# Reordering the opening of a routed expert kernel: exponentials behind four more evictions, copies on GpSimd, the first one-hot matrix ahead of the table, scatters regrouped

## The chip, the cores and the metric

The kernel runs on one core of one Trainium2 chip. The metric is device time in microseconds (us). Before the change the median of three runs is 1338.36 us (1338.25 to 1338.87). The profiled execution has a span of 1355.9 us; times inside the kernel are counted from the start of that span.

The engines are TensorE (PE; its weight loads are listed as PEld), VectorE (DVE), ScalarE (ACT), GpSimd (POOL) and SyncE (SP, which here only issues DMAs and reads registers). Each engine runs its own queue in order; they wait for each other through semaphores.

## What is computed

The input has 8 sequences of 3584 tokens of 192 floats. First a causal convolution over 7 taps, with softmaxed taps of one of 8 heads for each group of 24 channels. Then every token goes to one of 8 experts:

```python
logits = x @ w_gate;  local_gate = sigmoid(x @ w_local)
e = argmax(logits[s]) if s == 0 or local_gate[s] < 0.5 else prev_e   # carries along the sequence
p = softmax(logits[s])
out[s] = p[e] * (relu(x[s] @ w1[e]) @ w2[e])        # w1: 192 x 1024, w2: 1024 x 192
```

All of it is float32. The choice carries on from token to token, so routing is a scan along the sequence.

## The kernel before

**Parts and blocks.** The 28672 tokens are handled in 16 parts of 1792. A part is convolved, its logits are formed, it is routed (each token gets a row in a table of slots in DRAM, sorted by expert), and its rows are scattered into `slots` by GpSimd's indirect DMAs (`put`, line 761; 16 scatters for each of the first two parts). The expert work goes block by block: a block is 128 (later 256) tokens of one expert. For a block, SyncE loads the expert's weights (`load_w`, line 890, 1536 KB, into one of four `wb` buffers) and the rows from `slots` (`load_rows`, line 900). TensorE then turns the rows (`turn`), multiplies by w1 (`hidden`, line 951) and by w2 (`output`, line 968), and the result is scattered to the output.

**The opening.** The first two parts are convolved another way, on TensorE with a banded matrix: `wide` (line 191) is a generator with 23 yields that makes 16 matmuls of one head and one half each (`convolve`, line 203), turns the result (`turned`), copies some columns (`again`, line 217), and multiplies by the gate (`products`). In part 0 (`both` true) ScalarE and VectorE share the evictions from PSUM and GpSimd makes the copies of `again`. In part 1 (`both` false) ScalarE makes all evictions and the copies too. `wide_route` (line 391) is a second generator that routes such a part: the maximum of the logits, `ex = lg - max`, the keys (line 412 reads `ex`), the exponential on ScalarE that writes over `ex` (line 415), a transpose on TensorE (line 422), the scans over tokens on VectorE (lines 435 to 448), a transpose back (line 450), one-hot experts and their counts (lines 460 to 465), the running count `upto` (line 472), and the slot of each token, `pos`.

The driver (line 1058 on) interleaves them by hand. This order is the order of every engine's queue, since the scheduler is manual:

```python
for n in (7, 5, 1, 0, 0):
    next(route0)          # one stage of the routing of part 0
    some(wide1, n)        # n pieces of the convolution of part 1
puts_behind(None, 4)      # four scatters of part 0
rest(route0)              # first_table, hots(0)
some(wide1, WIDE - 17)
```

**The first table.** `first_table` (line 496) turns the counts into the table of the first blocks: which rows and which expert block i has (`tabi`, line 518). SyncE reads `tabi` before it can issue `load_w` for blocks 0, 1 and 2 (nine DMAs, line 897). The second half of the function forms `rel`, from which `hots(0)` (line 538) makes a one-hot matrix in four instructions. With it TensorE gathers the rows of block 0 straight from the chip's own memory (`gather`, line 544), with no detour through `slots`. Block 1 is gathered the same way with `hots(1)`.

**The scatters.** The 16 scatters of part 0 stand on GpSimd's queue in five groups. Four come first; then three behind the logits of part 1 (`mark["lt", 1]`, line 271), two behind `nf` (line 435), two behind `oh` (line 460) and five behind `upto` of part 1 (line 472). `load_rows` of block 2, the first that reads `slots`, waits for all 16. On SyncE's queue the weights of block 3 stand behind that load.

**PSUM buffers.** The matmuls of the opening all write to a pool of four `hps` buffers. TensorE's queue is in order, so a matmul that waits for a buffer to be evicted holds back every later one, those of the routing included.

Of the kernel before, what the change touches and what calls it, by code (L numbers as in the profile page):

```python
# [17 lines left out]
P = 128  # L18
# [5 lines left out]
UT = 128  # L24
# [42 lines left out]
def bcast(ap, n):  # L67

    return ap.rearrange("p (a o) -> p a o", o=1).to_broadcast([ap.shape[0], ap.shape[1], n])
# [8 lines left out]
def kernel(  # L78
# [112 lines left out]
    def wide(g, xv, y_sb, both):  # L191

        lps = yps_p.tile([P, 512], F32, name="yps")[:, :4 * TB].rearrange("p (q s) -> p q s", s=TB)
        count = [0]

        def mine():
            count[0] += 1  # L200
            return both and count[0] % 2 == 0

        def convolve(half, heads):
            bs = slice(half * NH, (half + 1) * NH)
            for h in heads:
                ps = hps_p.tile([P, 512], F32, name="hps")[:TB, :NH * GS]
                nc.tensor.matmul(ps, lhsT=hank[:NI, h, :],  # L207
                                 rhs=xv[:NI, bs, h * GS:(h + 1) * GS], start=True, stop=True)
                to = y_sb[:TB, bs, Y0 + h * GS:Y0 + (h + 1) * GS]
                at = ps.rearrange("p (b d) -> p b d", d=GS)  # L210
                if mine():
                    nc.vector.tensor_scalar(to, at, rz[:TB, h:h + 1], None, Alu.mult)
                else:
                    nc.scalar.activation(to, at, Act.Copy, scale=rz[:TB, h:h + 1])  # L214
                yield

        def again(half):
            bs = slice(half * NH, (half + 1) * NH)
            copy = nc.gpsimd.tensor_copy if both else nc.scalar.copy
            copy(yr[:, bs, :], y_sb[:TB, bs, Y0 + P:Y0 + D])  # L220
            copy(y_sb[:TB, bs, Y0 + D:IX], y_sb[:TB, bs, Y0:Y0 + DR])

        def turned(half, qs):
            at = half * 3 * NH // 2
            for q in qs:
                tps = hps_p.tile([P, 512], F32, name="hps")[:, :4 * TB].rearrange(
                    "p (u s) -> p u s", s=TB)
                for u in range(4):
                    b = half * NH + (q * 4 + u if q < 2 else 2 * u)
                    src = (y_sb[:TB, b, Y0:Y0 + P] if q < 2  # L230
                           else yr[:, b:b + 2, :].rearrange("p b d -> p (b d)"))
                    nc.tensor.transpose(tps[:, u, :], src, identity=ident[:TB, :TB])
                leave = nc.vector.tensor_copy if mine() else nc.scalar.copy
                leave(yT[:, at + 4 * q:at + 4 * q + 4, :], tps)
                yield

        def products():
            for j in range(4):
                u = j // 2 * 3 * NH // 2 + j % 2 * 4
                nc.tensor.matmul(lps[Q * j:Q * j + Q], lhsT=wgb[:, 0, :], rhs=yT[:, u:u + 4, :],  # L240
                                 start=True, stop=False, skip_group_check=True)
            for i in range(2):
                for j in range(4):
                    u = j // 2 * 3 * NH // 2 + NH + j % 2 * 2
                    nc.tensor.matmul(lps[Q * j:Q * j + Q, i::2, :], lhsT=wgb[:, 1 + i, :],
                                     rhs=yT[:, u:u + 2, :], start=False, stop=(i == 1),
                                     skip_group_check=True)

        yield from convolve(0, range(H))
        zy = z_tile()  # L250
        yT = zy[:, :3 * NH * TB].rearrange("p (u s) -> p u s", s=TB)
        yr = zy[:TB, 3 * NH * TB:].rearrange("p (b d) -> p b d", d=DR)
        again(0)
        yield from convolve(1, range(5))
        yield from turned(0, (0, 1))
        yield from convolve(1, range(5, H))
        yield from turned(0, (2,))
        again(1)
        yield from turned(1, range(3))
        products()  # L260
        if both:
            nc.vector.tensor_copy(lsb[:, :2, :], lps[:, :2, :])
            nc.scalar.copy(lsb[:, 2:, :], lps[:, 2:, :])
        else:
            nc.scalar.copy(lsb, lps)
        yield
        ltp = yps_p.tile([P, 512], F32, name="yps")[:TB].rearrange("p (q c) -> p q c", c=P)
        for q in range(4):
            nc.tensor.transpose(ltp[:, q, :], lsb[:, q, :], identity=ident)
        lt = sm.tile([P, NB, E + 1], F32, name="lt")[:TB]  # L270
        mark["lt", g] = nc.vector.tensor_copy(lt.rearrange("p (j q) e -> p j q e", q=4),
                              ltp.rearrange("p q (j c) -> p j q c", c=Q)[:, :, :, :E + 1])
        got[g] = lt
# [117 lines left out]
    def wide_route(g, y_sb, lt):  # L391
# [15 lines left out]
        nc.vector.tensor_reduce(mx, lg, axis=AX.X, op=Alu.max)  # L407
        ex = sm.tile([P, NB, E], F32, name="ex")[:TB]
        nc.vector.tensor_tensor(ex, lg, bcast(mx, E), op=Alu.subtract)

        eq = sm.tile([P, NB, E], F32, name="eq")[:TB]
        nc.vector.scalar_tensor_tensor(eq, ex, 0.0, bcast_mid(ed[:TB], NB), Alu.is_equal, Alu.mult)
# [73 lines left out]
        yield  # L486
        if g == 0:
            first_table(upto[:, :, NB], pos)
            hots(0)
        nc.vector.tensor_copy(place, upto[:, :, NB])  # L490
        nc.vector.tensor_tensor(base, place, eo, op=Alu.subtract)
        if g:
# [3 lines left out]
    def first_table(upto, pos):  # L496


        end, size = ends[0], 1
        ni = sm.tile([P, E], I32, name="ni")  # L500
        nc.vector.tensor_tensor(ni, upto, eo, op=Alu.subtract)
        nc.vector.tensor_scalar(ni, ni, UT.bit_length() - 1, None, Alu.arith_shift_right)
        new = sm.tile([P, E], F32, name="new")
        nc.vector.tensor_copy(new, ni)
        nc.vector.tensor_tensor_scan(end[:, 1:], new, new, 0.0, Alu.add, Alu.max)
        nc.vector.tensor_scalar(end[:, 1:], end[:, 1:], float(ONE[0]), None, Alu.min)
        inn = sm.tile([P, E], F32, name="inn")
        nc.vector.tensor_scalar(inn, end[:, :E], i_of, None, Alu.is_le)
        nc.vector.scalar_tensor_tensor(inn, end[:, 1:], i_of, inn, Alu.is_gt, Alu.mult)

        row = sm.tile([P, E], F32, name="row")
        nc.vector.tensor_tensor(row, eb, end[:, :E], op=Alu.subtract)
        add = sm.tile([P, 3, E], F32, name="add")
        nc.vector.scalar_tensor_tensor(add[:, 0, :], row, i_of, inn, Alu.add, Alu.mult)
        nc.vector.tensor_tensor(add[:, 1, :], ef, inn, op=Alu.mult)
        nc.vector.tensor_reduce(tab[0][:, 0:2], add[:, :2, :], axis=AX.X, op=Alu.add)
        ti = cst.tile([P, 2], I32, name="tabi0_0")
        nc.vector.tensor_copy(ti, tab[0][:, 0:2])
        tabi[0, 0] = ti

        inn = sm.tile([P, 2, E], F32, name="inn2", bufs=1)
        gt = sm.tile([P, 2, E], F32, name="gt2", bufs=1)
        nc.vector.tensor_tensor(inn, bcast_mid(end[:, :E], 2), which, op=Alu.is_le)
        nc.vector.tensor_tensor(gt, bcast_mid(end[:, 1:], 2), which, op=Alu.is_gt)
        nc.vector.tensor_tensor(inn, inn, gt, op=Alu.mult)
        nc.vector.tensor_tensor(gt, which, bcast_mid(row, 2), op=Alu.add)
        nc.vector.tensor_tensor(gt, gt, inn, op=Alu.mult)
        r2 = sm.tile([P, 2], F32, name="r2", bufs=1)
        nc.vector.tensor_reduce(r2, gt, axis=AX.X, op=Alu.add)
        rel = sm.tile([P, 2, NB], F32, name="rel", bufs=1)[:TB]  # L530
        nc.vector.scalar_tensor_tensor(rel, bcast(r2[:TB], NB), -float(UT), bcast_mid(pos, 2),
                                       Alu.mult, Alu.add)
        rels.append(rel)
        nc.vector.tensor_tensor(used, end[:, 1:], end[:, :E], op=Alu.subtract)

    rels = []
# [1 line left out]
    def hots(i):  # L538
        for b in range(0, NB, NB // 4):
            bs = slice(b, b + NB // 4)  # L540
            nc.vector.tensor_tensor(hot[:TB, i, bs, :], bcast(rels[0][:, i, bs], UT),
                                    bcast_mid(slot[:TB], NB // 4), op=Alu.is_equal)
# [519 lines left out]
    rest(wide0)  # L1062
    x_in[2] = load_x(2)
    route0 = wide_route(0, ya, got.pop(0))
    for n in (7, 5, 1, 0, 0):
        next(route0)
        some(wide1, n)

    def puts_behind(ins, n):
        for _ in range(n):  # L1070
            put(ins)

    puts_behind(None, 4)
    rest(route0)
    some(wide1, WIDE - 17)

    wbs, xgs = {}, {}

# [26 lines left out]
    rest(wide1)  # L1105
    puts_behind(mark["lt", 1], 3)
    route1 = wide_route(1, yb, got.pop(1))
    next(route1)
    hots(1)
    gather(0, ya, picks[0], range(4, NB))  # L1110
    next(route1)
# [10 lines left out]
    step(2.4)  # L1122
    xgs[1] = gathered(picks[1])
    next(route1)
    puts_behind(mark["upto", 1], 5)
    rest(route1)
    for i, (_, n, _, _) in enumerate(blocks):
        st["block"] = i
# [93 lines left out]
```

## Time and profile before

| | before |
|---|---|
| time, median of 3 | 1338.36 us |
| span of the profiled execution | 1355.9 us |
| TensorE busy | 1328.3 us (98%) |
| VectorE busy | 776.4 us (57%) |
| ScalarE busy | 514.1 us (38%) |
| GpSimd busy | 491.3 us (36%) |

The table is a mean over very different stages. From 200 us to the end TensorE is busy for 1145 of 1156 us; the change touches only what is queued in about the first 55 us. So the stages are read apart: in a table by stage, the columns are a stretch of the span, its length, the busy time of each engine with the number of its instructions, the granted TensorE clock (1.00 is full), the share of the DMA engines' time in use, and GB/s. In a timeline a line gives start, duration, engine, source line, operation, and in brackets how long the engine had been idle before and what ended that. A recorded matmul's end is modelled. The page's chain of what ended last has only the last output scatter in it, and tells nothing of the opening.

### The profile page before, as it was taken

The page shows a single profiled execution, that of the slowest core. Times are in us where ns is not written, and L with a number is a line of the kernel's source. Part 1 is how long each engine was busy: PE and PEld are TensorE (multiplying, and loading weights), DVE is VectorE, ACT ScalarE, POOL GpSimd, SP SyncE. Part 2 cuts the span into 40 slices and gives each one's busy share as a digit, 9 for nine tenths or more (in the row PEclk, how much of TensorE's full clock was granted, in tenths as well). Part 3 has the DMA queues.
Part 4 walks back from the last instruction along what each step waited for, and adds up shares of the span by engine and source line. Part 5 has one row for each costly group of instructions (what it writes and reads, how often), then busy time and mean ns, then how long its engine had stood idle before and what let it go on. Part 6 is the DMA issues. An engine that isn't in the chain of part 4 may idle for free. (4 is left out here: it accounts for less than half of the span.)

```text
span 1355.9 us, 41868 instructions
## 1 busy us (share of the span) xinstructions
PE 1328.3 (98%) x17140; PEld 1277.4 (94%) x17140; DVE 776.4 (57%) x2414; ACT 514.1 (38%) x1151; POOL 491.3 (36%) x534
## 2 busy tenths in 40 slices
PE   8889999999999999999999999999999999999998
PEld 7779999999999999999999999999999999999997
DVE  5858887887777777777786868786520000000000
ACT  6234444444343333333333343333333333333333
POOL 3543433434343434343434343434344211121111
PEclk9999999999999999999999999999999999999999
DMA  5789999977575757575757575756566555556993
GB/s 196 279 324 360 377 346 355 366 284 278 192 279 192 288 198 283 202 275 202 275 206 272 205 274 203 282 203 231 203 232 230 207 182 182 187 185 232 321 324 128
DMA packets 67299, 340.39 MB, mean 251 GB/s; under 512 B 12576, under 2 KB 23191, under 8 KB 47650
## 3 DMA queue, kind: packets, MB, share of 16 engines
q1 hardware_dynamic: 44784, 284.88, 58.8%
q0 software_dynamic: 22320, 52.82, 10.3%
q8 instruction: 136, 2.23, 0.6%
q14 instruction: 57, 0.47, 0.1%
q10 hardware_dynamic: 2, 0.00, 0.0%
HBM read 284.73 MB, written 53.41 MB: 249 GB/s over the span
## 5 line engine op out<-in xcount | busy, mean ns | idle before, releaser
L968 PE MATMUL yps<-wb,hT 64*128 64x192 f32 x7328 | 644.8, 326 | 8.6 <-ACT hT L956 5.6
L951 PE MATMUL hps<-xT,wb 64*128 64x256 f32 (+1 forms) x6816 | 636.4, 337 | 6.4 <-issue 5.0
L968 PEld LDWEIGHTS yps<-wb,hT 64*128 64x128 f32 x7328 | 601.4, 187 | 20.1 <-ACT hT L956 11.3
L951 PEld LDWEIGHTS hps<-xT,wb 64*128 64x128 f32 x6816 | 588.4, 188 | 32.0 <-issue 7.7
L984 POOL DMA_INDIRECT out_dram<-o_sb,xg x229 | 232.1, 1013 | 620.8 <-DVE o_sb L980 557.5
L956 ACT ACTIVATE hT<-hps 128x512 f32<-128x512 f32 (+1 forms) x568 | 262.3, 512 | 403.9 <-PE hps L951 284.7
L385 DVE SCALAR_TENSOR_TENSOR y_sb<-x_sb,c,y_sb 128x336 f32<-128x336 f32 x672 | 377.2, 571 | 19.4 <-ACT y_sb L375 1.3
L980 DVE SCALAR_TENSOR_TENSOR o_sb<-yps,xg,o_sb 128x192 f32<-128x192 f32 x229 | 87.5, 414 | 498.4 <-ACT o_sb L976 484.3
L768 POOL DMA_INDIRECT slots<-y_sb,posi x228 | 229.4, 1006 | 220.3 <-ACT hT L956 102.8
L976 ACT ACTIVATE o_sb<-yps,xg 128x192 f32<-128x192 f32 x229 | 86.8, 418 | 386.1 <-PE yps L968 365.3
L937 ACT COPY xT<-xps 128x768 f32<-128x768 f32 (+1 forms) x142 | 96.9, 682 | 9.7 <-remote 4.9
L357 PEld LDWEIGHTS xps<-ident,xg 64*128 64x128 f32 x1374 | 73.4, 139 | 5.4
L357 PE MATMUL xps<-ident,xg 64*128 64x64 f32 x1374 | 73.6, 222 | 0.0
L375 ACT ACTIVATE y_sb<-x_sb,c 128x336 f32<-128x336 f32 x112 | 64.6, 588 | 0.0
L563 DVE STREAM_TRANSPOSE z<-y_sb 128x768 f32<-128x768 f32 (+1 forms) x56 | 45.4, 853 | 0.4
L589 DVE COPY lt<-lq 32x36 f32<-32x36 f32 x224 | 40.6, 181 | 3.5
L573 PE MATMUL hps<-z,wg 64*32 64x128 f32 x1344 | 24.5, 272 | 1.0 <-issue 1.0
L573 PEld LDWEIGHTS hps<-z,wg 64*32 64x32 f32 x1344 | 19.1, 105 | 3.7 <-issue 2.7
L207 PE MATMUL hps<-x_sb,wb 118*112 118x192 f32 x64 | 12.5, 332 | 1.9 <-ACT y_sb L214 1.9
L581 DVE STREAM_TRANSPOSE lq<-ls 128x256 f32<-128x256 f32 x14 | 6.2, 444 | 12.8 <-ACT ls L578 12.8
L559 POOL COPY y_sb<-y_sb 128x896 f32<-128x896 f32 x14 | 13.3, 953 | 0.0
L665 DVE COPY bk<-so_far 1x32 f32<-1x32 f32 x56 | 12.3, 220 | 0.7
(240 smaller groups left out, 366.3 us busy)
## 6 DMA issues: line engine op xcount, KB each, us to landing
wb<-in_w_dram SPq DMA_DIRECT2D x138, 1536.0 KB
x_sb<-in_x_dram SPq DMA_DIRECT2D x14, 1920.0 KB
xg<-slots SPq DMA_DIRECT2D x87, 259.0 KB
xg<-slots SPq DMA_DIRECT2D x53, 129.5 KB
wb<-in_w_dram SPq DMA_DIRECT2D x12, 512.0 KB
out_dram<-o_sb,xg POOLq DMA_INDIRECT x229
slots<-y_sb,posi POOLq DMA_INDIRECT x228
x_sb<-in_xb_dram SPq DMA_DIRECT2D x4, 768.0 KB
```

The lines of the kernel that those rows point to most:

```text
L357: nc.tensor.transpose(to, src[rows], identity=ident[rows, rows])
L375: nc.scalar.activation(cols(h), chans(h, 0), Act.Copy, scale=c[:, h, 0:1])
L385: nc.vector.scalar_tensor_tensor(cols(h), chans(h, k), c[:, h, k:k + 1], cols(h), Alu.mult, Alu.add)
L563: nc.vector.transpose(z[:, t:u, :], y_sb[:, t:u, Y0:Y0 + D])
L768: ins = nc.gpsimd.indirect_dma_start(out=slots[:, :], in_=rows, in_offset=None, out_offset=bass.IndirectOffsetOnAxis(ap=to, axis=0)).ins
L937: copied = nc.scalar.copy(to, at)
L951: nc.tensor.matmul(hps[half][:, j, w], lhsT=wb[rows, f0:f0 + P], rhs=xT[rows, d, w], start=(d == 0 and j == 0), stop=(d == KD - 1), skip_g ...
L956: relu = nc.scalar.activation(hT[:, m:m + 2, w], hps[half][:, :, w], Act.Relu)
L968: nc.tensor.matmul(yps[half][:, k * D:(k + 1) * D], lhsT=hT[rows, m, k * P:(k + 1) * P], rhs=wb[rows, WA + m * D:WA + (m + 1) * D], start= ...
L976: nc.scalar.activation(o_sb[:, k, :], y[k][0], Act.Copy, scale=xg[:, k, 0:1])
L980: nc.vector.scalar_tensor_tensor(o_sb[:, k, :], y[k][1], xg[:, k, 0:1], o_sb[:, k, :], Alu.mult, Alu.add)
L984: sent = nc.gpsimd.indirect_dma_start(out=out, in_=o_sb[:, k, :], in_offset=None, out_offset=bass.IndirectOffsetOnAxis(ap=xg.bitcast(I32)[ ...
```

## The change

Four edits, all in the opening:

1. `wide_route` yields once more, after `ex` is formed and ahead of the keys and the exponential. The driver fills it with four pieces of part 1, so that four evictions that stood behind the exponential on ScalarE's queue now stand ahead of it. The three last pieces of the old second round go into an earlier round of the driver; the order on TensorE's queue stays.
2. `again` always copies on GpSimd. Four copies of part 1 leave ScalarE for GpSimd, ahead of the first scatter.
3. In `first_table` the way to `rel` and `hots(0)` comes first, and the way to `tabi`, which lets the weight loads start, comes behind it.
4. The scatters of part 0 are grouped 5, 3, 2, 2, 4 rather than 4, 3, 2, 2, 5.

```diff
         def again(half):
             bs = slice(half * NH, (half + 1) * NH)
-            copy = nc.gpsimd.tensor_copy if both else nc.scalar.copy
-            copy(yr[:, bs, :], y_sb[:TB, bs, Y0 + P:Y0 + D])
-            copy(y_sb[:TB, bs, Y0 + D:IX], y_sb[:TB, bs, Y0:Y0 + DR])
+            nc.gpsimd.tensor_copy(yr[:, bs, :], y_sb[:TB, bs, Y0 + P:Y0 + D])
+            nc.gpsimd.tensor_copy(y_sb[:TB, bs, Y0 + D:IX], y_sb[:TB, bs, Y0:Y0 + DR])
...
         nc.vector.tensor_tensor(ex, lg, bcast(mx, E), op=Alu.subtract)
+        yield
...
         if g == 0:
             first_table(upto[:, :, NB], pos)
-            hots(0)
...
+        row = sm.tile([P, E], F32, name="row")
+        nc.vector.tensor_tensor(row, eb, end[:, :E], op=Alu.subtract)
+        # in2, gt, r2 and rel, moved up unchanged from the end of the function
...
+        rels.append(rel)
+        hots(0)
+
         inn = sm.tile([P, E], F32, name="inn")
         # inn, add, the reduction into tab[0] and the cast into tabi follow, unchanged
...
-    for n in (7, 5, 1, 0, 0):
+    for n in (4, 3, 5, 1, 3, 0):
         next(route0)
         some(wide1, n)
...
-    puts_behind(None, 4)
+    puts_behind(None, 5)
     rest(route0)
-    some(wide1, WIDE - 17)
+    some(wide1, WIDE - 20)
...
-    next(route1)
+    some(route1, 2)
     hots(1)
...
-    puts_behind(mark["upto", 1], 5)
+    puts_behind(mark["upto", 1], 4)
```

## The prediction

> **What bounds the kernel now.** I read the table by stage first, because the busy shares of the whole span say only that TensorE is at 98%.
>
> ```profile
> 18.20:34.50 16.30, 12.84 (x96) 9.92 (x95) 12.47 (x52) 9.85 (x24) 5.58 (x9) 1.00 0.22 62
> 45.20:48.20 3.00, 1.85 (x27) 1.63 (x26) 2.86 (x8) 0.55 (x2) 1.80 (x3) 1.00 0.96 376
> 48.20:57.60 9.40, 7.77 (x76) 6.03 (x78) 8.64 (x34) 2.15 (x6) 5.08 (x6) 0.90 0.28 84
> 57.60:98.30 40.70, 35.09 (x516) 32.42 (x514) 23.11 (x42) 12.86 (x34) 22.22 (x23) 0.94 0.89 325
> 200.00:1356.00 1156.00, 1145.42 (x14702) 1108.60 (x14702) 624.54 (x1939) 431.68 (x929) 404.60 (x402) 1.00 0.67 240
> ```
>
> From 200 us on TensorE is all but full and no edit touches it: whatever the opening saves reaches the end only as an earlier start. Between 48.2 and 57.6 us the DMA engines are nearly empty (0.28, 84 GB/s) and then full again (0.89). SyncE's queue in the timeline tells why:
>
> ```profile
> 30.66 5.42 SPq L897 DMA_DIRECT2D wb<-in_w_dram  x9
> 55.82 1.19 SPq L904 DMA_DIRECT2D xg<-slots  x2
> 57.62 1.39 SPq L897 DMA_DIRECT2D wb<-in_w_dram  x3
> ```
>
> Weights of blocks 0 to 2 are issued from 30.66 us; then SyncE stands at the rows of block 2 until 55.82, and the weights of block 3 behind it. The rows wait for the last of 16 scatters, which starts at 53.04:
>
> ```profile
> 48.05 0.94 POOL L768 DMA_INDIRECT slots<-y_sb,posi  x1 [0.90 <-DVE upto L472]
> 49.29 0.94 POOL L768 DMA_INDIRECT slots<-y_sb,posi  x1 [0.30 <-issue]
> 53.04 0.94 POOL L768 DMA_INDIRECT slots<-y_sb,posi  x1 [0.30 <-issue]
> ```
>
> The first of the last five is released by `upto` of part 1 (DVE, 47.34 + 0.43 us). From 34.5 us to there VectorE's queue has no idle time (10.08 busy of the 10.7 us up to 45.2, 2.86 of the next 3.0), so `upto` is as early as VectorE gets to part 1. What held it up before:
>
> ```profile
> 19.27 0.31 ACT L415 ACTIVATE ex<-ex 112x128 f32<-112x128 f32 x1 [1.28 <-DVE eq L412]
> 19.95 1.23 PE L207 MATMUL hps<-x_sb,wb 118*112 118x192 f32 x6 [0.81 <-ACT y_sb L214]
> 20.91 0.62 ACT L220 COPY z<-y_sb 112x512 f32<-112x512 f32 x1
> 22.42 0.90 PE L207 MATMUL hps<-x_sb,wb 118*112 118x192 f32 x4 [1.06 <-ACT y_sb L214]
> 24.38 0.13 PEld L450 LDWEIGHTS hps<-ident,run 16*112 16x112 f32 x1 [0.24 <-ACT z L234]
> 24.64 0.29 DVE L460 TENSOR_TENSOR oh<-hps,en 112x128 f32<-112x128 f32 x1 [1.10 <-PE hps L450]
> 34.49 0.31 DVE L271 COPY lt<-yps 112x144 f32<-112x144 f32 x1 [0.42 <-PE yps L269]
> ```
>
> ScalarE idles 1.28 us for the exponential; TensorE has no free PSUM buffer meanwhile (0.81), then again while ScalarE makes the two copies (1.06), and the routing's transposes stand behind those matmuls. VectorE pays: 1.10 us before `oh` and 0.42 before `lt`.
>
> **What the Trainium skill says.** "GPSIMD Engine Reference", section 1, has GpSimd share SBUF interfaces with VectorE, with contention when VectorE's instruction has two SBUF inputs. The trace has the copy on both engines: 0.61 to 0.62 us on GpSimd (part 0), 0.62 on ScalarE (part 1), so the move costs nothing in itself; contention in part 1 no run shows yet. "TensorE: Matmul & The Clock Gate", part 1, says an idle window of about 3.4 us halves the clock. The trace agrees: TensorE is busy 1.96 of 3.5 us at 52.3 to 55.8, and from 55.8 to 59.2 us the clock is 0.51. "ScalarE: Activation LUTs", on table sets, says copies lie in every set; the trace has one table load, at 1.35 us, so reordering exponential and evictions adds none.
>
> **The change part by part.**
>
> *Exponential.* The evictions run on from 17.99 us at the pace of their matmuls (8 records in 1.47 us, ending 19.14), the fourth is done at about 19.6, and the exponential takes 19.6 to 19.9, instead of 19.27 to 19.58. That is 0.3 us late for the sum on VectorE (line 426), whose three instructions (19.75 to 20.53) then end at 20.75. TensorE, no longer held, goes from 19.14 straight on: 6 records of 1.23 us, then the transpose, done at about 20.75 instead of 21.37. So `nf` moves from 21.41 to about 20.75: 0.66 us.
>
> *Copies.* Two copies cost ScalarE 20.91 to 21.96, 1.05 us, and two more the same at 26.97. Without them evictions of part 1 are some 2.3 us ahead (1.28 + 1.05), so TensorE is free when `run` is ready: 2.13 us after `nf` starts (21.41 to 23.54), at 22.9. The transpose back starts at 22.95 instead of 24.38: **1.4 us**, which includes the 0.66. If a buffer still held TensorE, only 0.7 remains. I take 1.4: by my count of the matmuls ahead of it (4 records 0.8, 8 records 0.96, 2 records 0.4) TensorE is free at about 22.8. On GpSimd the four copies (4 x 0.6) come before the first scatter, which needs `posi` in any case; the second pair waits for an eviction that ends at about 25 us, so GpSimd is free at 26.3, ahead of the scatters' data. If contention doubled them, 27.5: the first scatter (28.58 before) still fits, at about 27.3 to 27.8.
>
> *First one-hot matrix.* Line 472 moves from 25.83 to 24.4. Seven small instructions leave the way to `hots(0)`: 28.55 to 28.96, 29.16 to 29.78, and 0.12 for `used`, together 1.15 us. `hots(0)` starts at 24.4 + (31.15 - 25.83) - 1.15 = 28.6 instead of 31.15, and the transposes behind the first gathers come earlier too, so VectorE no longer waits at `lt` of part 1: **0.4 us**. VectorE's work up to there is the same, hence no more than that. The price: `tabi` is cast after four one-hot instructions (2.5 us) and six small ones (1.1), at 28.6 + 3.6 = 32.2 instead of 29.87, so weights start 2.3 us later, at 33.0. Behind them wait the DMA engines only: 4.7 MB took 30.7 to about 48.2 us, so they end at 50.6. Block 0, now at about 43.4, needs its third by about 40; block 1 needs its own by 45 and starts at about 52.5. The idle DMA stretch hides it. I cost this at nothing; the upper end is the full 2.3.
>
> *Scatters.* Each takes 1.25 us from start to start (48.05, 49.29). One fewer behind `upto` is **1.25 us**. The fifth in the first group ends at about 33.6 us, when `lt` of part 1 is due (34.49 + 0.31 - 1.8 = 33.0), so it pushes the next groups 0.6 us, and the 3 us hole before the `oh` group (44.81, idle 2.97) absorbs that.
>
> *Sum.* The last scatter moves by 1.4 + 0.4 + 1.25 = 3.1 us, from 53.04 to about 49.9. Rows of block 2 and weights of block 3 follow, at about 52.7 and 54.5, after the first weights have landed (50.6). Block 0 itself starts only 1.8 us earlier (45.22 to 43.4), but TensorE crawls through the end of it (8 matmuls in 52.3 to 55.8) for as long as scatters run, so I let block 1 follow them. From there the order is unchanged: 1338.36 - 3.1 = **1335.3**.
>
> **The rivals.**
>
> *The shift gains a clock step too.* A shorter stall in block 0 leaves no idle window, and the 3.4 us at half clock, worth 1.7, go away: 1333.6. For: the clock fell right after that stall. Against: a second drop, at 83 to 86.5 us, shows that such stalls recur.
>
> *Only part of it arrives.* TensorE's block 0 sets the pace, not the scatters, or the stage 57.6 to 98.3 (DMA 0.89) absorbs some: 1.8 us or less, 1336.6. For: TensorE has 35.09 of 40.70 us busy there. Against: loads there start with the rows that the scatters release.
>
> *The late weights become the bound.* Scatters and weights now overlap to 50.6 us; only about 2 us of the idle DMA stretch is left at 52.7. If the loads end later than I think, or the rows queue behind them, the 2.3 us arrive at the end and the gain does not: 1340.7, slower.
>
> **How the numbers follow.** Full shift 0.45, with the clock step 0.20, part 0.20, late weights 0.15. Likeliest: 1335.3. The bound for "faster" by 0.2% is 1335.7, so the full shift passes it barely; I put 0.38 of its 0.45 there, with all of the clock case: 0.58. Slower is the last case, 0.15; within 0.2% is what remains, 0.27. The range leaves out the late weights and the tail of the clock case: 1332.0 to 1339.0; it holds the loss of 0.7 in the copies and some of a late load.
>
> **What would show it.** In the changed profile: no idle time before the exponential on ScalarE and none for TensorE on line 207 near 20 and 22 us; line 450 near 23; `upto` of part 1 near 45.5; the last scatter of part 0 near 50; rows of block 2 near 52.7; weights from 33. If rows and the weights of block 3 come 3 us earlier but the block after 98 us does not, the second rival holds. A wait for weights in blocks 0 to 2 shows the third. I am wrong altogether if the stage from 57.6 to 98.3 has a bound of its own.

## The result, and the profile after

The first comparison gave 1337.88 us (1336.85 to 1338.86, 4 runs) against 1338.61 (4 runs): a ratio of 0.9995, interval 0.9977 to 1.0012. It cannot tell the forecast of 1335.3 (0.9977) from no change. Repeated with more runs beside it, the changed kernel took 1336.10 us (10 runs) against 1338.44 (35 runs): 0.9980, interval 0.9970 to 0.9989. So the change is worth about 0.2%, some 2.5 us: between the 2.3 us by which the medians differ and the 2.7 us of the ratio.

The profile of before in the prediction is of an execution of 1357.64 us, and the two last jobs below found every kernel, the one before too, near 1357 us, while all other runs were at 1331 to 1343. Before and after are therefore compared with a second profile of the kernel before, called "before again" (span 1336.2 us).

The same stages as in the prediction, from the table by stage of the changed kernel (stretch, length, busy time of each engine, clock, DMA share, GB/s):

```profile
18.20:34.50 16.30, 13.99 (x111) 11.86 (x110) 13.55 (x54) 8.85 (x23) 8.32 (x14) 1.00 0.19 66
45.20:48.20 3.00, 1.81 (x29) 1.65 (x29) 2.85 (x7) 0.66 (x2) 1.80 (x3) 1.00 1.03 417
48.20:57.60 9.40, 7.95 (x124) 7.79 (x124) 8.64 (x33) 3.80 (x11) 4.16 (x5) 1.00 0.60 194
57.60:98.30 40.70, 35.56 (x570) 34.41 (x568) 27.83 (x71) 13.81 (x39) 22.63 (x23) 0.92 0.92 362
```

The DMA engines, nearly empty from 48.2 to 57.6 us before (0.28, in before again too), are now busy for 0.60 of it: the late weights fill the first part, and the next loads come earlier. The opening, in the timeline of the changed kernel:

```profile
20.79 0.30 ACT L415 ACTIVATE ex<-ex 112x128 f32<-112x128 f32 x1
18.96 2.44 PE L207 MATMUL hps<-x_sb,wb 118*112 118x192 f32 x14
24.05 0.19 PE L450 MATMUL hps<-ident,run 16*112 16x16 f32 x1 [0.58 <-DVE run L448]
26.27 0.75 POOL L219 COPY z<-y_sb 112x512 f32<-112x512 f32 x1 [4.11 <-DVE at L476]
26.99 0.63 DVE L482 CAST posi<-pos 112x16 int32<-112x16 f32 x1
```

The exponential starts with no idle time before it, TensorE's 14 matmuls on line 207 are one group without a hole, and the transpose back (line 450) waits for its data instead of a PSUM buffer. The last line is a surprise, taken up below. Then SyncE's queue and the last scatters:

```profile
34.77 5.83 SPq L898 DMA_DIRECT2D wb<-in_w_dram  x9
54.34 1.18 SPq L905 DMA_DIRECT2D xg<-slots  x2
56.14 1.39 SPq L898 DMA_DIRECT2D wb<-in_w_dram  x3
```

```profile
47.82 0.94 POOL L769 DMA_INDIRECT slots<-y_sb,posi  x1 [0.89 <-DVE upto L472]
51.56 0.94 POOL L769 DMA_INDIRECT slots<-y_sb,posi  x1 [0.30 <-issue]
```

The weights went back, the rows came forward, and four scatters instead of five follow `upto`. The starts must not be compared as they stand: the convolution's first matmul came at 6.48 us in before again, 7.47 in this execution and 6.51 in another of the changed kernel. TensorE was busy up to it in the first two, and the matmuls ahead of it, which the change does not touch, were slower in this execution: the last four of line 152 took 1.17 us, and 0.66 in the two others. Counted from that first matmul:

| start of | before again | changed | changed, again | shift | forecast |
|---|---|---|---|---|---|
| transpose back, part 0 (L450) | 18.22 | 16.58 | 17.13 | -1.6, -1.1 | -1.4 |
| `upto` of part 0 (L472) | 19.67 | 17.99 | 18.53 | -1.7, -1.1 | -1.4 |
| first scatter | 22.42 | 21.20 | 21.73 | -1.2, -0.7 | -0.8 to -1.3 |
| first weights | 24.48 | 27.30 | 27.84 | +2.8, +3.4 | +2.3 |
| `upto` of part 1 | 40.70 | 39.65 | 40.21 | -1.1, -0.5 | -1.8 |
| last scatter of part 0 | 46.40 | 44.09 | 44.65 | -2.3, -1.7 | -3.1 |
| rows of block 2 | 49.26 | 46.88 | 47.45 | -2.4, -1.8 | -3.1 |
| weights of block 3 | 51.06 | 48.68 | 49.25 | -2.4, -1.8 | -3.1 |
| rows of block 7 | 86.24 | 83.11 | 83.86 | -3.1, -2.4 | (unchanged order) |

The shift is there at every station, smaller than forecast from `upto` of part 1 on, and not lost by block 7.

### The profile page after: what moved, and what is told of

Read it like the earlier page. It is cut to its first block, busy times and chain, and to the rows that moved or that the text cites. A ratio compares the mean times of both kernels' runs of the same rounds, so it can differ in the third digit from the quotient of the medians.

```text
span 1335.1 us, 41872 instructions
## 1 busy us (share of the span) xinstructions
PE 1314.4 (98%) x17140; PEld 1256.5 (94%) x17140; DVE 775.9 (58%) x2414; ACT 510.6 (38%) x1147; POOL 493.3 (37%) x538
## 5 line engine op out<-in xcount | busy, mean ns | idle before, releaser
L969 PE MATMUL yps<-wb,hT 64*128 64x192 f32 x7328 | 632.0, 325 | 0.2 <-issue 0.2
L952 PE MATMUL hps<-xT,wb 64*128 64x256 f32 (+1 forms) x6816 | 626.2, 336 | 4.7 <-ACT ls L579 3.0
L952 PEld LDWEIGHTS hps<-xT,wb 64*128 64x128 f32 x6816 | 563.4, 187 | 44.6 <-ACT ls L579 3.2
L356 PEld LDWEIGHTS xps<-ident,xg 64*128 64x128 f32 x1374 | 67.3, 139 | 11.8 <-DMA xg<-slots 2.4
L356 PE MATMUL xps<-ident,xg 64*128 64x64 f32 x1374 | 68.7, 222 | 3.5 <-DMA xg<-slots 3.5
L548 PE MATMUL yps<-y_sb 112*128 112x194 f32 x64 | 11.5, 331 | 1.8 <-DVE y_sb L542 1.8
L548 PEld LDWEIGHTS yps<-y_sb 112*128 112x128 f32 x64 | 10.4, 189 | 2.6 <-DVE y_sb L542 2.0
```

The costliest lines, as they stand in the source:

```text
L356: nc.tensor.transpose(to, src[rows], identity=ident[rows, rows])
L952: nc.tensor.matmul(hps[half][:, j, w], lhsT=wb[rows, f0:f0 + P], rhs=xT[rows, d, w], start=(d == 0 and j == 0), stop=(d == KD - 1), skip_g ...
L969: nc.tensor.matmul(yps[half][:, k * D:(k + 1) * D], lhsT=hT[rows, m, k * P:(k + 1) * P], rhs=wb[rows, WA + m * D:WA + (m + 1) * D], start= ...
```

## The experiments

Three theories were written down before the runs. A: the opening is earlier, but the stage up to 98 us has a bound of its own and absorbs it. B: the shift passes through, but the weights that edit 3 delays take it back. C: the parts add up and pass through unchanged. Each kernel was timed next to the kernel before.

**The kernel before, once more**, for a second profile and for the scatter of its times.

> The kernel before once more, for a second profile of it. Its first profile had a span of 1355.9 us against 1338.4 timed, so some of its waits on TensorE between 48 and 98 us may belong to that execution alone. Both theories: ratio 1.000 within 0.001. If that profile was an exception, the span is now near 1337, the 8 slow matmuls at 52 to 56 us are gone, and block 1 starts on TensorE near 53.5 and not at 55.85; the last scatter of part 0 still starts 45.7 to 47 us after the first convolution matmul, and block 7 starts near 98.

1338.85 us (22 runs) against 1338.87 (51 runs, 1335.48 to 1342.63): 1.0002, interval 0.9994 to 1.0009. Single executions differ by up to 7 us, which is why four against four had not settled 2.5 us. Much of that scatter goes with TensorE's mean granted clock: of the 51 executions, the 11 with a clock of 0.993 took 1339.7 us on average, the 9 with 0.998 took 1336.5.

**Edits 1 and 2 alone** (exponential, copies).

```diff
-            copy = nc.gpsimd.tensor_copy if both else nc.scalar.copy
+            copy = nc.gpsimd.tensor_copy
...
         nc.vector.tensor_tensor(ex, lg, bcast(mx, E), op=Alu.subtract)
+        yield
...
-    for n in (7, 5, 1, 0, 0):
+    for n in (4, 3, 5, 1, 3, 0):
...
-    some(wide1, WIDE - 17)
+    some(wide1, WIDE - 20)
...
-    next(route1)
+    some(route1, 2)
```

> Only the first two edits: exponential behind four more evictions, copies of part 1 on GpSimd. Theory A (the opening gets earlier, but the stage to 98 us, full DMA queues and the waits they bring, absorbs it): upto of part 0 and the last scatter 1.4 to 1.8 us earlier counted from the first convolution matmul, block 7 on TensorE less than 0.7 us earlier, time within 1 us of before. Theory B (the shift does reach the end, and the late weights of the one-hot edit cancel it): 1.4 to 1.8 us faster, 1336.8.

1337.13 us (14 runs), 0.9990, interval 0.9981 to 0.9999: 1.3 us. From the first matmul on, `upto` of part 0 is 1.73 us earlier, `upto` of part 1 and the last scatter 1.3.

**Edit 3 alone** (first one-hot matrix ahead of the table).

```diff
             first_table(upto[:, :, NB], pos)
-            hots(0)
...
         rels.append(rel)
+        hots(0)
+
+        # inn, add, tab[0] and tabi, moved down unchanged from above row
```

> Only the third edit: rel and hots(0) ahead of the table. Weights issued about 3.6 us later than before (30.7 to about 34.3), scatters at most 0.4 us earlier. Theory A: within 1 us of before, since the rows of block 2 and not the first weights release the stage after. Theory B: 2 us slower or more, 1340.5.

1338.03 us (14 runs), 1.0000, interval 0.9989 to 1.0011. Weights are issued at 34.87 us instead of 30.96, `upto` of part 1 and the last scatter stand where they stood, to 0.1 us; the rows of block 2 come 0.2 us later. It neither helps nor costs by more than the interval, 1.5 us either way.

**Edit 4 alone** (scatters 5, 3, 2, 2, 4).

```diff
-    puts_behind(None, 4)
+    puts_behind(None, 5)
...
-    puts_behind(mark["upto", 1], 5)
+    puts_behind(mark["upto", 1], 4)
```

> Only the fourth edit: scatters grouped 5, 3, 2, 2, 4. The last scatter starts 1.25 us earlier and the rows of block 2 are issued 1.2 us earlier. Theory A: time within 0.7 us of before, block 7 where it was. Theory B: 1.2 us faster, 1337.2.

1336.64 us (14 runs), 0.9990, interval 0.9980 to 1.0000. From `upto` of part 1 to the last scatter it is 4.44 us instead of 5.70, the 1.25 of the forecast. (In the profiled execution TensorE ran at half clock for 3.4 us from 23.0, in the middle of part 0's routing, so its absolute stations are some 1.6 us late.)

1.3 + 0 + 1.3 us is 2.6, as theory C has it. But the intervals reach from 0.1 to 2.5 us for edits 1 and 2 and from 0 to 2.7 for edit 4, and there is a rival: the clock. Its mean over the executions was 0.9951 for the kernel before, 0.9952 with edits 1 and 2, 0.9958 with edit 3 and 0.9967 with edit 4. What remains at the same clock I estimate by a straight line fitted to all times of this job, with one slope for the clock (0.57 us for each us of clock that is not granted) and one step for each kernel: 1.2 us for edits 1 and 2 (standard error 0.3), nothing for edit 3 (0.3), 0.6 for edit 4 (0.3). So the gain of edits 1 and 2 stands by itself. That edit 4 moves the scatters by 1.25 us is shown; that this shift reaches the end is not. More than half of its gain may be the clock, by chance or because a shorter wait leaves fewer half-clock stretches, and no run tells these apart.

The second job put the whole beside the whole without edit 3.

**The changed kernel once more.**

> The changed kernel once more, for a tighter time than the four runs gave (1337.88, interval 0.9977 to 1.0012). Theory C (the parts add up: ScalarE edits alone gave 0.9990, the regrouping alone 0.9990, the one-hot edit alone 1.0000, each within about 0.001; a shift of the scatters passes through the full DMA stretch unchanged): ratio 0.9980, about 1336.2. Theory A (the stage to 98 us or what follows takes most of it back): ratio 0.9993 or above, 1338.

1336.10 us, 0.9980, as above. Theory A expected 0.9993 or more, outside the interval. The clock differs here too, 0.9969 on average against 0.9950; the same fit to this job (slope 0.34) leaves an estimated 2.0 us (standard error 0.5) at the same clock.

**The changed kernel with the table first** (edit 3 undone).

```diff
             first_table(upto[:, :, NB], pos)
+            hots(0)
...
         rels.append(rel)
-        hots(0)
-
-        # inn, add, tab[0] and tabi, moved back up above row
```

> The changed kernel with the third edit undone: table and weights first, one-hot matrix behind. Weights from about 29.5 us and not 34.8; last scatter at most 0.4 us later than in the changed kernel. Theory C: same time as the changed kernel within 0.7 us, since the rows of block 2 release the stage after in both. Theory B (late weights cost): 1.5 to 2 us faster than the changed kernel.

1335.72 us (22 runs), 0.9980, interval 0.9974 to 0.9987. The weights are back at 30.32 us, 4.0 earlier, and the time is the same to within about 1 us (an estimated 2.3 us below before at the same clock, standard error 0.3): theory B, which expected 1.5 to 2 us from this, falls, and a gain from edit 3 is not seen.

**Still fewer scatters at the end** (5, 3, 3, 3, 2 on the changed kernel).

```diff
-    puts_behind(mark["nf", 1], 2)
+    puts_behind(mark["nf", 1], 3)
...
-    puts_behind(mark["oh", 1], 2)
+    puts_behind(mark["oh", 1], 3)
...
-    puts_behind(mark["upto", 1], 4)
+    puts_behind(mark["upto", 1], 2)
```

> The changed kernel with scatters of part 0 grouped 5, 3, 3, 3, 2: two fewer behind upto of part 1. The last scatter starts about 1.9 us earlier than in the changed kernel (51.6 to about 49.7, counted in that profile). Theory C: rows of block 2, weights of block 3, rows of block 7 each 1.5 to 2 us earlier, time 1.5 to 2 us lower than the changed kernel. Theory A: rows of block 2 earlier, block 7 and the time unchanged within 0.7.

1335.73 us (8 runs), 0.9974, interval 0.9963 to 0.9984: no difference from the changed kernel that could be told. The last scatter starts at 48.76 us, 2.4 earlier than in the changed kernel of the same job, yet the rows of block 2 come only 0.43 earlier. SyncE's queue and the table by stage of this kernel:

```profile
53.52 1.18 SPq L905 DMA_DIRECT2D xg<-slots  x2
```

```profile
48.00:50.00 2.00, 2.00 (x35) 2.00 (x34) 1.69 (x10) 1.03 (x3) 1.40 (x2) 1.00 1.03 413
50.00:52.00 2.00, 2.00 (x33) 2.00 (x31) 1.79 (x12) 0.69 (x2) 0.00 (x0) 1.00 0.51 169
52.00:54.00 2.00, 2.00 (x38) 1.94 (x34) 1.89 (x5) 0.88 (x4) 0.00 (x0) 1.00 0.02 5
```

The last scatter has been issued for two microseconds while the weights still fill the DMA engines (1.03), and the packets drain up to about 52 us. From the last scatter to the rows it takes 4.8 us here, 2.8 in the changed kernel. My reading was that the scatters now wait behind the weights that edit 3 made late; the kernel that was to show it, with the table first, follows below, and speaks against it.

**The next wait in the stage up to 98 us.** The rows of block 7 are read from `slots` as soon as the 32nd scatter has landed. That one starts at 81.8 us, but the rows come at 90.37, when a full stretch of the DMA engines ends. The largest thing queued there is the load of the input of part 3 (1920 KB, issued at 65.5 us in block 3), so it was put off to block 6, on the changed kernel. The convolution of part 3 starts later with it: `LATE` sets both.

```diff
-    LATE = 3
+    LATE = 6
```

> The changed kernel with the 1920 KB load of part 3 issued at block 6 and not at block 3, so out of the full DMA stretch between 58 and 90 us; the convolution of part 3 starts later with it. Theory C: that stretch is bound by the bytes in it, so the rows of block 7, which wait for the last scatter of part 1 to land, come 4 to 5 us earlier (1920 KB at about 400 GB/s) and the time falls by 2 to 4 us unless the late convolution costs it back. Theory A in the form that scatters or VectorE set that stretch: rows of block 7 within 1 us of where they are (90.6).

1331.69 us (5 runs), 0.9943, interval 0.9930 to 0.9956: 4.4 us below the changed kernel, and 6.8 below before. The rows of block 7 on SyncE's queue, TensorE's wait for them, and the DMA engines while the 32nd scatter lands, first in the changed kernel of the same job, then with the later load:

```profile
90.37 1.23 SPq L905 DMA_DIRECT2D xg<-slots  x2
...
92.46 0.40 PE L356 MATMUL xps<-ident,xg 64*128 64x64 f32 x6 [3.97 <-DMA xg<-slots]
...
82.00:86.00 4.00, 2.88 (x109) 2.49 (x96) 0.00 (x0) 0.00 (x0) 2.65 (x3) 1.00 1.00 415
```

```profile
85.55 1.24 SPq L905 DMA_DIRECT2D xg<-slots  x2
...
87.68 0.41 PE L356 MATMUL xps<-ident,xg 64*128 64x64 f32 x6 [0.95 <-DMA xg<-slots]
...
82.00:86.00 4.00, 3.19 (x77) 2.80 (x62) 1.15 (x5) 1.30 (x5) 2.55 (x4) 1.00 0.40 137
```

The share falls from 1.00 to 0.40 and the rows move by 4.8 us. TensorE waits 0.95 us for them instead of 3.97, and never falls to half clock before the end. The clock was 0.999 in all five executions, against 0.995 to 0.998 in the changed kernel, so 1.0 to 1.6 us of the 4.4 come by way of the clock (an estimate: 0.999 - 0.9969 is 0.0021 of 1336 us, times the two slopes). How much the load and how much the later convolution give was not separated.

**Everything that had helped together**: table first, scatters 5, 3, 3, 3, 2, without and with the later load.

> The changed kernel with the table built first again (third edit undone) and the scatters of the first part spread as 5, 3, 3, 3, 2. With the one-hot matrices first and the same spread, the last scatter of the first part started at 48.8 us instead of 51.2, but the rows of block 2 were gathered only 0.43 us earlier (53.5 us), while the weights issued at 33.8 us kept the DMA engines full until about 51 us. If the scatters' bytes wait behind those late weights, the weights here issue near 30 us, the queue is empty by about 47 us, and the rows of block 2 are issued near 51.5 us: ratio 0.996, 1.5 to 2 us below the same spread with the late weights. If something other than the weights sets the rows, they stay near 53.5 us and the ratio is 0.9975, as it was there. The absorbing theory (the stage up to 98 us takes up what the opening gains) expects 0.9975 in either case, with the rows of block 7 unmoved near 89.6 us.

1356.94 us (14 runs) against 1358.80 for the kernel before (27 runs): 0.9989, interval 0.9981 to 0.9997.

> The same kernel (table first, scatters 5, 3, 3, 3, 2) with the load of the second part's x put off from block 3 to block 6. The later load alone, on the changed kernel, took 4.4 us (ratio 0.9943, rows of block 7 at 85.6 instead of 90.4 us). If the two gains lie in different stretches and add, rows of block 7 near 83.5 to 84 us and ratio 0.9925 to 0.993; if the earlier opening is absorbed, 0.994 with the rows of block 7 near 85.5 us.

1356.59 us (14 runs), 0.9985, interval 0.9974 to 0.9995. Since the kernel before itself took 20 us more than in the other jobs, both were run again.

> The same kernel as in the run before it (changed, table first, scatters 5, 3, 3, 3, 2), once more: there the kernel before itself took 1358.8 us instead of 1338.4, TensorE stood in waits called issue between 52 and 98 us, and the DMA engines moved some 345 GB/s where full instead of 390, so that it said nothing of the question. With the kernel before at 1338 to 1339 us again: if the scatters' bytes wait behind the late weights, rows of block 2 near 51.5 us and a ratio of 0.996; if something else sets the rows, 53.5 us and 0.9975. With the kernel before near 1358 again: 0.9989 again, since the stage up to 98 us is then TensorE's own.

1358.89 us (14 runs) against 1358.22 (27 runs): 1.0008, interval 0.9996 to 1.0020. The expectation of 0.9989 again was a miss.

> The same kernel as in the run before it (table first, scatters 5, 3, 3, 3, 2, load of the second part's x at block 6), once more. With the kernel before at 1338 to 1339 us: if the gains of the two stretches add, rows of block 7 near 83.5 to 84 us and ratio 0.9925 to 0.993; if the earlier opening is absorbed there, 85.5 us and 0.994. With the kernel before near 1358: 0.9985 again, the later load worth nothing, since block 7 then waits for TensorE and not for its rows.

1356.55 us (14 runs), 0.9988, interval 0.9977 to 0.9999. It was 0.9988 for 0.9985 expected.

So the question of these four runs, whether the two gains add and what sets the rows of block 2, stays open. One thing they do show: SyncE's load of the rows still waits for nothing but the scatters, and from the start of the last one to the rows it takes 3.2, 2.7, 4.7 and 4.4 us, though the table is first and the DMA engines are busy for no more than 0.38 of any two microseconds from 48 to 54. Late weights are not needed to make a scatter land late. The rest is a kernel with other limits. The table by stage from 98 to 300 us, for before again and then for the first of the four:

```profile
98.00:300.00 202.00, 201.80 (x3161) 198.83 (x3161) 176.67 (x557) 88.04 (x233) 84.44 (x84) 0.99 0.95 366
```

```profile
98.00:300.00 202.00, 195.76 (x3112) 185.69 (x3094) 167.82 (x539) 83.71 (x226) 78.77 (x77) 1.00 0.93 348
```

TensorE's weight loads are busy for 13 us less and the DMA engines move 5% less at nearly the same share. The opening differs too. VectorE at the routing of part 1 in the first of the four:

```profile
39.69 0.26 DVE L435 COPY nf<-hps 16x112 f32<-16x112 f32 x1 [1.69 <-remote]
```

It has no idle time there in the changed kernel with the table first at 1336 us; here it waits 1.69 us (0.9 to 1.2 in the three others), and `upto` of part 1 starts 41.2 us after the first matmul in all four runs, as in the prediction's profile of before (47.34 - 6.16), though `upto` of part 0 is 1.7 us earlier. In the later load's first run block 7's rows come at 90.4 us, 4.2 before those of the kernel without it, but TensorE enters block 7 only at 104.1:

```profile
104.07 2.84 PE L951 MATMUL hps<-xT,wb 64*128 64x128 f32 x48
```

There the absorbing theory holds: TensorE, not the rows, is late. The timeline puts most of its stops up to there down to "issue", that is, to nothing that the profile shows. Why the DMA engines are slower and why TensorE stops was not found.

## Why the prediction was nearly right

The time is right to about 0.8 us (1336.10 and 1335.3) by the repeat; by the first comparison it was 2.6 us off. That the gain would pass 0.2%, which the prediction held likelier than not (0.58), is not shown: 0.9995 at first, then 0.9980, which is the bound itself. The main line of the mechanism held: an earlier routing of part 0, one scatter fewer, and so earlier rows of block 2. One term was nothing, one was cut down on its way, and one reason was wrong. By its own steps:

- **Exponential.** Right. `nf` starts 0.87 us earlier (15.24 to 14.37 after the first matmul; forecast 0.66), with no wait on either engine. In the other execution of the changed kernel it was 0.33, for a reason told under the copies. Edits 1 and 2 were run only together, so the time of each alone is not known.
- **Copies, the 1.4 us.** Right at the transpose back (1.6 us) and at `upto` of part 0 (1.7 us). But the step carried that figure unchanged to part 1, and there it is 1.3 in the run of these two edits alone. The missing 0.4 us is contention, which the prediction had bounded for GpSimd's copies only, not for VectorE's work beside them. The cast of `posi` (L482) falls into a copy on GpSimd and takes 0.63 us, not the 0.17 of before again:

```profile
27.68 0.17 DVE L482 CAST posi<-pos 112x16 int32<-112x16 f32 x1
```

  VectorE's queue has no hole after it, so all that follows is 0.45 us late: 1.7 - 0.45 is the 1.3 measured. Once it hit the routing itself, in the second profile of the changed kernel, where line 416 (0.17 us in the first) met the first copy of part 1. This is VectorE, then GpSimd:

```profile
20.07 0.59 DVE L416 SCALAR_TENSOR_TENSOR fc<-key,fr 112x16 f32<-112x16 f32 x1
```

```profile
20.02 0.61 POOL L219 COPY z<-y_sb 112x512 f32<-112x512 f32 x1 [0.22 <-ACT y_sb L214]
```

  It ends with the copy, and every station of that execution up to block 7 is 0.5 to 0.8 us later. The Trainium skill has this in "SBUF — State Buffer", under "Who interferes with whom": the port pair that VectorE and GpSimd share is an exclusive lock held for a whole instruction, not a bandwidth that is split. Both lines agree: they are lengthened to about the end of the copy, by 0.42 to 0.46 us. By the same section not every VectorE instruction takes that lock: one with two SBUF inputs does, like line 416, and a cast can. The prediction named the first kind only, and so looked past line 482, which has one input. An instruction of another kind, in a copy of the first execution (21.55 to 22.16 us), took the 0.25 us that it takes in before again:

```profile
21.66 0.25 DVE L428 RECIPROCAL rs<-rs 112x16 f32<-112x16 f32 x1
```

- **First one-hot matrix, the 0.4 us.** Wrong: it is 0. The step rested on one line, VectorE idle for 0.42 us before `lt` of part 1. In before again that idle time is not there:

```profile
34.33 0.31 DVE L271 COPY lt<-yps 112x144 f32<-112x144 f32 x1
```

  It seems to belong to the condition in which the prediction's profile was taken: of the five executions profiled near 1357 us four have such a gap (0.36 to 0.65 us), of the nine profiled near 1336 none. Edit 3 alone left `upto` of part 1 in place (40.73 and 40.70 after the first matmul). Its price, costed at nothing, was indeed hidden to within the interval of that run, though the weights came 2.8 to 3.4 us later and not 2.3: the 0.45 us of the cast is in that too.
- **Scatters, the 1.25 us.** Right to 0.01 us for the scatters; at the end of the kernel, shown only within the limits told above.
- **The sum.** 1.25 + 0 + 1.25 is 2.5 us where the prediction had 3.1. What was mis-sized is the 1.4 (it arrives as 1.25) and the 0.4 (nothing). The last scatter moved by 2.3 us in one execution and 1.7 in the other.
- **From the scatters to the end.** The reason given was wrong, and the outcome right. That TensorE crawls through the end of block 0 for as long as scatters run, so that block 1 follows them, was read from the prediction's profile; in before again block 1 starts before the last scatter does:

```profile
52.25 1.95 PE L951 MATMUL hps<-xT,wb 64*128 64x128 f32 x31
52.88 0.94 POOL L768 DMA_INDIRECT slots<-y_sb,posi  x1 [0.30 <-issue]
```

  That the sum came out near the time all the same is luck in this step. What follows the scatters is block 2, through its rows. TensorE's wait for them in before again, and in the changed kernel:

```profile
57.92 0.40 PE L357 MATMUL xps<-ident,xg 64*128 64x64 f32 x6 [2.75 <-DMA xg<-slots]
```

```profile
56.55 0.40 PE L356 MATMUL xps<-ident,xg 64*128 64x64 f32 x6 [1.45 <-DMA xg<-slots]
```

  Block 2 starts at 60.8 and 59.4 us. Two waits for rows, at blocks 2 and 7 (there 5.27 us in before again, 2.10 and 3.97 in the changed kernel), are what hand the shift on, as the traces read; no run took one of them away by itself.
- **The rivals.** "Late weights become the bound" fell: undoing edit 3 changed nothing that could be told. In "only part of it arrives" the 57.6 to 98.3 stage was to absorb some; it did not at 1336 us, and the shift was smaller already at `upto` of part 1. "A clock step too" was meant for the drop at 55.8 us, and before again has none there: its only one ahead of the end is 6.8 us from 93.9, in the wait for block 7. Drops of 3.4 to 10.2 us came and went between executions of much the same kernel. Over many executions, though, the changed kernel did have the higher clock, 0.9969 against 0.9950, so this rival is in part true: 2.0 us are left of 2.8 (the difference of the means) at the same clock. With the table first the clock was 0.9957 and 2.3 us are left of 2.6. The prediction also took TensorE's 1.96 busy us of 3.5 ahead of its drop as agreeing with the idle window that it cites for a halved clock; a window busy for more than half is not idle, and other drops in these runs came after the like.

## What to carry to other kernels

Follow an expected shift station by station, each against a fixed point of the same execution (here the first matmul); a term that rests on one idle gap in one profile needs a second profile before it is counted. Look at the granted clock beside the times before two small gains are added up. A copy moved to GpSimd is free only if VectorE's instructions beside it are not on the path: look for what falls into the copy's time. When an edit's gain is used up, ask what the next wait's data stand behind: a load put off by three blocks gave 4.4 us where four edits of the opening gave 2.5.

## What the runs showed of the hardware that was not expected

- A tiny VectorE cast, or one of two inputs (112 x 16), that falls into a GpSimd copy of about 0.6 us takes 0.59 to 0.63 us instead of 0.17; a reciprocal of that size in such a copy took its usual 0.25.
- A scatter can land late. Rows that wait for the 32nd scatter come 8.6 us after it starts at a DMA share of 1.00, and 4.4 us after (81.16 to 85.55) where the share falls to 0.40. But the 16th took 4.7 us at a share of 0.38 or less in one execution near 1357 us, and 2.8 in the changed kernel, so a full share is not the only cause.
- TensorE's clock fell to half after stretches in which TensorE was far from idle: it was busy for 1.54 of the 3.4 us ahead of the drop at 23.0 us (edit 4 alone) and for 2.06 of the 3.4 us ahead of one at 72.9 us (the later load, first job near 1357 us).
- The same kernel can take 20 us more for a whole job, with 3 to 5% less DMA throughput from 98 to 300 us and TensorE stops that no wait explains. There the waits that an edit removes are not the ones that bind: the later load, worth 4.4 us at 1336 us, gave 0.3 us in one of the jobs there (1356.94 to 1356.59) and 2.3 in the other (1358.89 to 1356.55).
